# A chunk-selecting attention kernel with a routed expert layer: key transposes moved, one score unit split over column tiles, chunk sums at full height

## The chip, the cores and the metric

The kernel runs on one core of one Trainium2 chip. The metric is the device time of one execution in microseconds (us). The compute engines of the core run beside each other and wait for one another through semaphores: TensorE (PE; its weight loads are PEld), VectorE (DVE), ScalarE (ACT), GpSimd (POOL). SyncE (SP) issues transfers.

## The reference, cut to what matters

Attention first, for 4 batches of 8 heads with 768 positions of 64 numbers. Keys are cut into 24 chunks of 32. For each query an upper bound of its score with each chunk is made from the chunk's least and greatest key; the 6 best causal chunks are kept, and the softmax runs over these alone. Then every token (512 numbers, 3072 tokens) goes to the one of 8 experts that its gate prefers.

```python
k_chunks = k.reshape(B, H, nc, chunk, D)
k_min, k_max = np.min(k_chunks, axis=3), np.max(k_chunks, axis=3)
ub = np.sum(np.maximum(q[..., None, :] * k_min[:, :, None], q[..., None, :] * k_max[:, :, None]), axis=-1)
top_chunks = np.argsort(np.where(causal, ub, -1e9), axis=-1)[..., -6:]
scores = np.where(sel & causal_positions, scale * q @ k.T, -1e9)
attn_out = softmax(scores) @ v
# ...
expert_idx = np.argmax(x @ w_gate, axis=1)
out[tokens of e] = gate * (np.maximum(x @ w1[e], 0) @ w2[e])
```

Since max(q a, q b) = (q (a + b) + |q| |a - b|) / 2, the bound is made (twice as large, which changes no order) by two matmuls: q with the chunk sums max + min, and |q| with the chunk differences max - min.

## The kernel before: the parts that the change touches

The attention goes over 16 pairs of heads. The main loop runs through pair i in four groups g of work, and prepares the next pairs in between: `prep` steps of pair i+1 (bounds `ub`, `select`, `mask`) and of pair i+2 (transposes of k and q, and `kse`, the chunk sums), and router steps of earlier pairs. The order of the instructions of TensorE, GpSimd and SyncE is that of the program text. VectorE and ScalarE are put in order by the scheduler of the kernel's framework, which goes by the order in the text and by when it reckons that the inputs are there; only at the start and in the last pair do they, too, follow the text.

The tiles with tag "m" are PSUM tiles of a pool with three buffers, those with tag "s" (scores) have two, and "o" (output) one. The steps of `prep`, indented less, and the score units:

```python
    def k_half(hf):
        if hf == 0:
            s["kmx"] = work.tile([128, NCH], FP32, tag="kmx", name="kmx")
            s["kmn"] = work.tile([128, NCH], FP32, tag="kmn", name="kmn")
        pt = ps_m.tile([128, 384], FP32, tag="m")
        for t in range(3):
            nc.tensor.transpose(pt[:, ts(t, 128)], s["k"][:, 3 * hf + t], ident_f[:])
        pk = pt[:].rearrange("p (c w) -> p c w", w=CH)
        nc.vector.tensor_reduce(s["kmx"][:, ts(hf, 12)], pk, AX.X, ALU.max)
        nc.vector.tensor_reduce(s["kmn"][:, ts(hf, 12)], pk, AX.X, ALU.min)
        nc.scalar.activation(kte[0:64, 0, ts(hf, 384)], pt[0:64, :], AF.Copy, bias=0.0, scale=0.125)
        nc.scalar.activation(kte[0:64, 1, ts(hf, 384)], pt[64:128, :], AF.Copy, bias=0.0, scale=0.125)

    def kse():
        for hd in range(2):
            r = slice(64 * hd, 64 * hd + 64)
            c = slice(32 * hd, 32 * hd + NCH)
            nc.vector.tensor_tensor(ks[r, c], s["kmx"][r, :], s["kmn"][r, :], ALU.add)
            nc.vector.tensor_tensor(kd[r, c], s["kmx"][r, :], s["kmn"][r, :], ALU.subtract)

    def ub():
        pu = ps_m.tile([128, 384], FP32, tag="m")
        for w_, nm in ((ks, "qT"), (kd, "qA")):
            x_ = s[nm][:].rearrange("p a c -> p (a c)")
            for h in range(2):
                nc.tensor.matmul(pu[64 * h:64 * h + 64, 0:320], lhsT=w_[:], rhs=x_[:, ds(128 + 320 * h, 320)],
                                 start=(nm == "qT"), stop=(nm == "qA"), skip_group_check=True)
        s["ubT"] = work.tile([128, 384], FP32, tag="ud", name="ubT")
        nc.scalar.activation(s["ubT"][:, 0:320], pu[:, 0:320], AF.Copy)


    def select():
        pt = ps_m.tile([128, 3, 2, 2, 32], FP32, tag="m")
        for t in range(3):
            nc.tensor.transpose(pt[:, t], s["ubT"][:, ds(c0s[t], 128)], ident_f[:])
        ubm = work.tile([128, 3, 2, 2, NCH], FP32, tag="ubm")
        nc.vector.tensor_tensor(ubm[:].rearrange("p n h d c -> p (n h) d c"),
                                pt[:].rearrange("p n h d c -> p (n h) d c")[:, :, :, 0:NCH],
                                cbias[:].rearrange("p n h c -> p (n h) c").unsqueeze(2)
                                .to_broadcast([128, 6, 2, NCH]), ALU.add)
        top8 = work.tile([128, 3, 2, 2, 8], FP32, tag="top8")
        for t in range(3):
            for hf in range(2):
                for hd in range(2):
                    nc.vector.max(out=top8[:, t, hf, hd], in_=ubm[:, t, hf, hd])
        u3 = ubm[:].rearrange("p a b c n -> p (a b c) n")
        t3 = top8[:].rearrange("p a b c n -> p (a b c) n")
        nc.vector.tensor_tensor(nsel[:].rearrange("p a b c n -> p (a b c) n")[:, :, 0:NCH], u3,
                                t3[:, :, TOPK - 1:TOPK].to_broadcast([128, 12, NCH]), ALU.is_lt)

    def mask():
        pt = ps_m.tile([64, S], BF16, tag="m")
        for hf in range(2):
            for t in range(3):
                nc.tensor.transpose(pt[:, ds(128 + 320 * hf + c0s[t], 128)],
                                    nsel[:, t, hf].rearrange("p a n -> p (a n)"), ident_b[:])
        nc.scalar.activation(qsb[64:64 + NCH, 0, 128:S], pt[0:NCH, 128:S], AF.Copy)
        nc.scalar.activation(qsb[64:64 + NCH, 1, 128:S], pt[32:32 + NCH, 128:S], AF.Copy)

    units = [(0, [(0, 384, 0)]), (0, [(1, 256, 0), (2, 128, 256)]),
             (1, [(0, 384, 0)]), (1, [(1, 384, 0)]), (1, [(2, 384, 0)]), (1, [(3, 384, 0)]),
             (1, [(4, 256, 0), (5, 128, 256)])]

    def scores(i, u):
        kte, qsb = KTE[i % 2], QSB[i % 2]
        qb, parts = units[u]
        ps = ps_s.tile([128, 2, 512], FP32, tag="s", name="ps")
        if u in (0, 2):
            P = work.tile([128, 2, 384], FP32, tag="Pa", bufs=4, name="Pa")
        else:
            P = work.tile([128, 2, 384], FP32, tag="Pr", bufs=4, name="Pr")
        st[i][f"P{u}"] = P
        pvs = []
        for n, (kb, w, c0) in enumerate(parts):
            if len(parts) == 1:
                pv = ps[:, :, 0:w]
            else:
                pv = ps[:, n, 0:2 * w].rearrange("p (a w) -> p a w", a=2)
            for hd in range(2):
                nc.tensor.matmul(pv[:, hd, :], lhsT=kte[:, hd, ts(kb, 128)],
                                 rhs=qsb[:, hd, ds(qb * 384 + 384 - w, w)],
                                 start=True, stop=True, skip_group_check=True)
            pvs.append(pv)
        for pv, (kb, w, c0) in zip(pvs, parts):
            nc.scalar.activation(P[:, :, ds(c0, w)], pv, AF.Exp)
        for n, (kb, w, c0) in enumerate(parts):
            if kb >= 3 * qb:
                pd = P[:, :, ds(c0, 128)]
                nc.gpsimd.affine_select(out=pd, in_=pd, pattern=[[0, 2], [1, 128]],
                                        compare_op=ALU.is_ge, fill=0.0, base=0, channel_multiplier=-1)

    def attend(i, u):
        s = st[i]
        qb, parts = units[u]
        P, vt = s[f"P{u}"], s["v"]
        first, last = u in (0, 2), u in (1, 6)
        if first:
            s["po"] = ps_o.tile([128, 384], FP32, tag="o", name="po")
        po = s["po"]
        for n, (kb, w, c0) in enumerate(parts):
            for hd in range(2):
                nc.tensor.matmul(po[64 * hd:64 * hd + 64, 384 - w:384], lhsT=vt[:, kb, hd, :],
                                 rhs=P[:, hd, ds(c0, w)], start=first,
                                 stop=last and n == len(parts) - 1, skip_group_check=True)
        if last:
            ot = work.tile([128, 384], FP32, tag="ot", bufs=3)
            nc.vector.tensor_copy(out=ot[:], in_=po[:])
            s[f"ot{qb}"] = ot
        if first:
            s[f"acc{qb}"] = P
        else:
            acc = s[f"acc{qb}"]
            for n, (kb, w, c0) in enumerate(parts):
                nc.vector.tensor_tensor(acc[:, :, 384 - w:384], acc[:, :, 384 - w:384],
                                        P[:, :, ds(c0, w)], ALU.add)
```

The ranking of the tokens of a batch, of which the loop runs one in the second pair of each batch after the first (pairs 5, 9 and 13):

```python
    def rank():
        oh = bst[b]["oh"]
        of = oh[:].rearrange("p u e -> p (u e)")
        pr = ps_m.tile([128, 128], FP32, tag="m")
        nc.tensor.matmul(pr[:, 0:48], lhsT=U128[:], rhs=of, start=True, stop=False,
                         skip_group_check=True)
        for u in range(1, 6):
            nc.tensor.matmul(pr[:, 8 * u:48], lhsT=ones_b[:], rhs=of[:, 0:48 - 8 * u],
                             start=False, stop=(u == 5), skip_group_check=True)
        for u in range(6):
            nc.tensor.matmul(pr[:, 64:64 + E], lhsT=ones_b[:], rhs=oh[:, u, :],
                             start=(u == 0), stop=(u == 5), skip_group_check=True)
        rk = work.tile([128, 6, E], FP32, tag="sh")
        nc.vector.tensor_tensor(rk[:], pr[:, 0:48].rearrange("p (u e) -> p u e", e=E),
                                base_e[:].unsqueeze(1).to_broadcast([128, 6, E]), ALU.add)
        nc.vector.tensor_tensor(rk[:], rk[:], oh[:], ALU.mult)
        sl = work.tile([128, 6], FP32, tag="sl")
        nc.vector.tensor_reduce(sl[:], rk[:], AX.X, ALU.add)
        sli = work.tile([128, 6], I32, tag="sli", bufs=2)
        nc.vector.tensor_copy(out=sli[:], in_=sl[:])
        nc.vector.tensor_tensor(base_e[:], base_e[:], pr[:, 64:64 + E], ALU.add)
        bst[b]["sli"] = sli
```

The loop, for one pair (cut after the scatters), where `groups` is (0, 1), (2, 3), (4, 5), (6,):

```python
    for g in range(4):
        if g == 0:
            scores(i, 2)
            scores(i, 3)
            run(rout, i - 2, "x1")
        elif g == 1:
            scores(i, 4)
            scores(i, 5)
            if hp == 1 and b > 0:
                route[b - 1][1]()
            run(prep, i + 1, "select")
        elif g == 2:
            scores(i, 6)
            if i == NP - 1:
                for j in range(XB, 2 * XB):
                    meta(j - XB)
                    gather(j)
                    if j < len(x_slots):
                        x_in(j)
            run(prep, i + 2, "k0")
            run(prep, i + 1, "mask")
        else:
            run(rout, i - 1, "lgp", "x0")
            if i + 1 < NP:
                scores(i + 1, 0)
                scores(i + 1, 1)
            run(prep, i + 2, "k1", "q0", "q0e", "q1")
            if i + 3 < NP:
                load(i + 3, "k", "q")
        for u in groups[g]:
            attend(i, u)
        if g == 3:
            run(prep, i + 2, "q1e", "kse")
        if g == 0:
            run(prep, i + 1, "ub")
            flush()
            if 0 < i < NP - 1:
                load(i + 1, "v")
        if g == 3 and hp == 0 and b > 0:
            flush(sums_)
            route[b - 1][0]()
        if g == 1:
            run(rout, i - 1, "ud")
        if 1 <= hp <= 2 and b > 0 and spread[4 * (hp - 1) + g]:
            route[b - 1][2](spread[4 * (hp - 1) + g])
# ...
```

## Time and profile before

| | |
|---|---|
| time, median of 3 runs | 360.15 us (359.7 to 360.66) |
| span of the profiled execution | 358.6 us |
| attention, pairs 0 to 15 | up to about 250 us |
| expert layer, TensorE busy in 19 to 20 of each 20 us | 260 to 340 us |
| mean granted TensorE clock | 0.992 of full speed |

The profile's page gives first the busy time of every engine, then groups of instructions by line. "L298" is line 298 of the kernel, the score matmul in `scores`; L303 is its exp, L307 the causal select, L320 the value matmul, L325 the eviction of its result, L332 the adding up of the weights; L205 to L210 are `k_half`, L215 to L227 the same for q, L233 and L234 `kse`, L241 and L244 `ub`, L249 to L262 `select`, L269 to L272 `mask`, L348 to L356 the router's sums `ud`, L361 to L388 `lgp` and `xr`, L432 to L448 `rank`, with `oh` made in L411. A timeline row has the start, the length, the engine, the line, what is written from what, and how many instructions are merged in it; in brackets stands the idle time ahead of it and what ended that. A matmul's shape is given as rows by columns of its weights, and then that of the moving operand. A busy TensorE is not TensorE at its peak, because the ends of pipelined matmuls are modelled; the starts are measured.

### The profile page before, as it was taken

Reading aid. Unit: us, or ns where it says so; the run is one execution under the profiler, and the core shown is the slowest. Engines: PE = TensorE matmul, PEld = TensorE weight load, DVE = VectorE, ACT = ScalarE, POOL = GpSimd, SP = SyncE. Lnnn points to the kernel's source line nnn. Section 1 sums busy time; section 2 is a strip of 40 time slices with the busy share of each in tenths; the row PEclk is TensorE's granted clock in tenths of the full one; section 3 lists DMA queues with packets and bytes.
Section 4 is the critical chain, followed back from the end, with each engine's and each line's share of the span. In section 5 each row is a group of like instructions: output and inputs, shape, how many; then the busy total and the mean of one; then the engine's idle time right before and its main releaser. Section 6 shows DMA issues by size and latency. Waiting matters only on the chain. (4 is left out here: it accounts for less than half of the span.)

```text
span 358.6 us, 7585 instructions
## 1 busy us (share of the span) xinstructions
PE 326.9 (91%) x2312; PEld 171.5 (48%) x2312; DVE 235.0 (66%) x815; ACT 231.2 (64%) x398; POOL 180.4 (50%) x296
## 2 busy tenths in 40 slices
PE   6679999999899999999999988998799999999990
PEld 5535455455455465554554545443344344444430
DVE  5799889889999898999988999846460000000000
ACT  2497797797687897867977967642344444445440
POOL 3075425445474453466534547575577665653331
PEclk9999999999999999999999999999999999999996
DMA  8619998999957999937989973476999999998851
GB/s 153 112 26 194 210 220 139 215 167 215 207 127 151 182 176 195 202 100 178 200 134 212 187 148 113 73 135 116 165 211 233 221 237 197 203 186 201 157 126 48
DMA packets 138215, 59.83 MB, mean 167 GB/s; under 512 B 122811, under 2 KB 131005, under 8 KB 138176
## 3 DMA queue, kind: packets, MB, share of 16 engines
q1 hardware_dynamic: 119072, 29.52, 45.4%
q0 software_dynamic: 17536, 29.42, 42.0%
q10 hardware_dynamic: 1568, 0.39, 0.6%
q8 instruction: 21, 0.34, 0.4%
q14 instruction: 18, 0.15, 0.2%
HBM read 56.14 MB, written 10.51 MB: 186 GB/s over the span
## 5 line engine op out<-in xcount | busy, mean ns | idle before, releaser
L332 DVE TENSOR_TENSOR Pa<-Pa,Pr 128x768 f32<-128x768 f32 (+2 forms) x112 | 81.6, 729 | 1.1
L307 POOL TENSOR_SCALAR_AFFINE_SELECT Pr<-Pr 128x256 f32<-128x256 f32 x80 | 33.5, 437 | 67.3 <-ACT Pr L303 66.1
L303 ACT ACTIVATE Pr<-ps 128x768 f32<-128x768 f32 (+2 forms) x112 | 65.0, 630 | 3.2 <-PE ps L298 2.9
L612 PE MATMUL py<-w_all,hT 128*128 x224 | 52.7, 379 | 2.7 <-DMA hT<-h__3653 1.9
L298 PE MATMUL ps<-QSB,KTE 128*128 128x384 bf16 (+2 forms) x288 | 50.4, 292 | 1.2 <-DVE QSB L711 0.2
L620 POOL DMA_INDIRECT out_dram<-y,ti_all x28 | 27.8, 993 | 30.2 <-ACT y L619 26.3
L298 PEld LDWEIGHTS <-KTE 128*128 128x128 bf16 x288 | 24.1, 97 | 27.3 <-issue 21.2
L612 PEld LDWEIGHTS <-hT 128*128 128x128 bf16 x224 | 21.8, 98 | 29.5 <-DMA hT<-h__3653 2.3
L619 ACT ACTIVATE y<-py,gt_all 128x512 f32<-128x512 f32 x27 | 18.6, 687 | 20.8 <-PE py L612 18.4
L454 POOL DMA_INDIRECT xs_dram<-xrow,sli x24 | 26.9, 1121 | 7.7 <-issue 5.0
L356 ACT ACTIVATE ud<-pu 128x384 f32<-128x384 f32 x16 | 7.9, 492 | 32.8 <-PE pu L353 30.7
L303 ACT ACTIVATE Pa<-ps 128x768 f32<-128x768 f32 x32 | 26.0, 812 | 3.8 <-PE ps L298 3.2
L601 PE MATMUL ph<-w_all,KTE 128*128 x120 | 28.4, 379 | 0.0
L169 POOL DMA_DIRECT2D w_all<-in_moe_w_dram x32 | 24.3, 760 | 0.0
L307 POOL TENSOR_SCALAR_AFFINE_SELECT Pa<-Pa 128x256 f32<-128x256 f32 x16 | 6.4, 398 | 35.3 <-ACT Pa L303 35.3
L601 PE MATMUL ph<-w_all,QSB 128*128 x96 | 22.7, 379 | 0.3 <-issue 0.3
L575 DVE TENSOR_TENSOR ti_all<-xgqA,inv_i 128x1 int32<-128x1 int32 x9 | 1.4, 159 | 29.6 <-DMA xgqA<-xs_dram,grow 29.6
L554 POOL DMA_INDIRECT xgqA<-xs_dram,grow x14 | 14.6, 1046 | 10.2 <-issue 3.3
L554 POOL DMA_INDIRECT xgqT<-xs_dram,grow x14 | 14.5, 1033 | 8.7 <-DVE gt_all L577 4.9
L325 DVE COPY ot<-po 128x384 f32<-128x384 f32 x32 | 17.7, 553 | 1.6 <-PE po L320 0.9
L575 DVE TENSOR_TENSOR ti_all<-xgqT,inv_i 128x1 int32<-128x1 int32 x8 | 1.3, 159 | 26.5 <-DMA xgqT<-xs_dram,grow 26.5
L226 POOL CAST QSB<-qT 64x384 bf16<-64x384 f32 x30 | 16.3, 551 | 4.1 <-DVE qT L224 2.8
(311 smaller groups left out, 665.0 us busy)
## 6 DMA issues: line engine op xcount, KB each, us to landing
w_all<-in_moe_w_dram POOLq DMA_DIRECT2D x32, 512.0 KB, 6.0
out_dram<-y,ti_all POOLq DMA_INDIRECT x28, 3.6
t__122<-in_k_dram SPq DMA_DIRECT2D x2, 192.0 KB, 3.5
t__125<-in_q_dram ACTq DMA_DIRECT2D x2, 192.0 KB, 4.0
t__128<-in_v_dram SPq DMA_DIRECT2D x2, 192.0 KB
t__196<-in_k_dram SPq DMA_DIRECT2D x2, 192.0 KB, 3.1
t__206<-in_q_dram SPq DMA_DIRECT2D x2, 192.0 KB, 3.8
t__209<-in_v_dram SPq DMA_DIRECT2D x2, 192.0 KB
```

Source lines behind the costliest of these rows:

```text
L169: nc.gpsimd.dma_start(out=dst, in_=src.rearrange("(c p) f -> p c f", p=128))
L298: nc.tensor.matmul(pv[:, hd, :], lhsT=kte[:, hd, ts(kb, 128)], rhs=qsb[:, hd, ds(qb * 384 + 384 - w, w)], start=True, stop=True, skip_grou ...
L303: nc.scalar.activation(P[:, :, ds(c0, w)], pv, AF.Exp)
L307: nc.gpsimd.affine_select(out=pd, in_=pd, pattern=[[0, 2], [1, 128]], compare_op=ALU.is_ge, fill=0.0, base=0, channel_multiplier=-1)
L325: nc.vector.tensor_copy(out=ot[:], in_=po[:])
L332: nc.vector.tensor_tensor(acc[:, :, 384 - w:384], acc[:, :, 384 - w:384], P[:, :, ds(c0, w)], ALU.add)
L454: d = nc.gpsimd.indirect_dma_start(out=xs_dram[:], out_offset=bass.IndirectOffsetOnAxis(ap=sli[:, u:u + 1], axis=0), in_=bst[b][f"xrow{u % ...
L554: d = nc.gpsimd.indirect_dma_start(out=xg_bufs[j % XB].bitcast(I32), out_offset=None, in_=xs_dram[:], in_offset=bass.IndirectOffsetOnAxis( ...
L601: nc.tensor.matmul(ph[:, fh, :], lhsT=xT[:, c, :], rhs=w_all[:, ds(wo + (c * F + fh * 512), 512)], start=(c == 0), stop=(c == NDC - 1), sk ...
L612: nc.tensor.matmul(py[:], lhsT=hT[:, c, :], rhs=w_all[:, ds(wo + (W1W + c * DM), DM)], start=(c == 0), stop=(c == NFC - 1))
L619: nc.scalar.activation(y[:], py[:], AF.Copy, bias=0.0, scale=fs[j]["gt"])
L620: d = nc.gpsimd.indirect_dma_start(out=out[:], out_offset=bass.IndirectOffsetOnAxis(ap=fs[j]["ti"], axis=0), in_=y[:], in_offset=None, bou ...
```

## The change

It has three parts, and a rewriting that makes them possible: every step that had matmuls and evictions in one function is cut into a matmul part (`_mm`), a VectorE part (`_v`) and a ScalarE part (`_a`), so that their order can be set one by one.

- **Key transposes.** The transposes of the first half of the keys of pair i+2 go from group 2, between the scores of unit 6 and the masks, to group 1, behind the transposes of the selection. In a ranking pair the rank matmuls now follow both; they stood ahead of the selection. The VectorE work is in the text in the order selection, rank, key reductions.
- **The last score unit.** Unit 6 is computed in halves of 64 keys, each a matmul of 64 weight columns into 64 partitions of PSUM: eight matmuls for four. [...] In units 1 and 6 the two parts of the scores now lie side by side for each head, so that one exp over 128x768 takes the place of two.
- **Chunk sums.** Two full-height operations make max + min and max - min of both heads, and a third multiplies both by a 0/1 mask of the heads `bm` into one tile of block form. There were four of half height.

The exponentials of the router's gate (`ex`) take a buffer with another tag, and its steps after the one-hot are a function of their own, `gates`, that comes after all of it.

The diff, cut to its core; `s`, `ts` and `ds` are as above, and what is left out only renames or cuts functions:

```diff
+        def kse():
+            kt2 = work.tile([128, 2, NCH], FP32, tag="top8", name="kt2")
+            nc.vector.tensor_tensor(kt2[:, 0], s["kmx"][:], s["kmn"][:], ALU.add)
+            nc.vector.tensor_tensor(kt2[:, 1], s["kmx"][:], s["kmn"][:], ALU.subtract)
+            nc.vector.tensor_tensor(ksd[:, :, :, 0:NCH], kt2[:].unsqueeze(2).to_broadcast([128, 2, 2, NCH]),
+                                    bm[:].unsqueeze(1).to_broadcast([128, 2, 2, NCH]), ALU.mult)
+
 # ...
-        def kse():
-            for hd in range(2):
-                r = slice(64 * hd, 64 * hd + 64)
-                c = slice(32 * hd, 32 * hd + NCH)
-                nc.vector.tensor_tensor(ks[r, c], s["kmx"][r, :], s["kmn"][r, :], ALU.add)
-                nc.vector.tensor_tensor(kd[r, c], s["kmx"][r, :], s["kmn"][r, :], ALU.subtract)
-
 # ...
-    def scores(i, u):
+    def scores(i, u, split=False):
         kte, qsb = KTE[i % 2], QSB[i % 2]
         qb, parts = units[u]
         ps = ps_s.tile([128, 2, 512], FP32, tag="s", name="ps")
+        n = 64 if split else 128
+        for kb, w, c0 in parts:
+            for hd in range(2):
+                for h in range(128 // n):
+                    nc.tensor.matmul(ps[ds(h * n, n), hd, ds(c0, w)], lhsT=kte[:, hd, ds(kb * 128 + h * n, n)],
+                                     rhs=qsb[:, hd, ds(qb * 384 + 384 - w, w)],
+                                     start=True, stop=True, skip_group_check=True)
 # ...
-        for pv, (kb, w, c0) in zip(pvs, parts):
-            nc.scalar.activation(P[:, :, ds(c0, w)], pv, AF.Exp)
-        for n, (kb, w, c0) in enumerate(parts):
+        nc.scalar.activation(P[:], ps[:, :, 0:384], AF.Exp)
+        for kb, w, c0 in parts:
 # ... in the loop, groups 1 and 2; groups 0 and 3 keep the order of their matmuls:
                 elif g == 1:
                     scores(i, 4)
                     scores(i, 5)
-                    if hp == 1 and b > 0:
-                        route[b - 1][1]()
-                    run(prep, i + 1, "select")
+                    run(prep, n, "sel_mm")
+                    run(prep, m, "k_mm", 0)
+                    if router:
+                        rank_mm()
+                    run(prep, n, "sel_v")
+                    if router:
+                        rank_v()
+                    run(prep, m, "k_v", 0)
+                    run(prep, m, "k_a", 0)
+                    av(i, 2)
+                    av(i, 3)
+                    add(i, 3)
+                    run(rout, i - 1, "ud")
                 elif g == 2:
-                    scores(i, 6)
+                    scores(i, 6, True)
 # ...
-                    run(prep, i + 2, "k0")
-                    run(prep, i + 1, "mask")
+                    run(prep, n, "mask")
+                    av(i, 4)
+                    av(i, 5)
+                    add(i, 4)
+                    add(i, 5)
 # ... and at the end of group 3 (av, o_ev and add are attend, cut in three):
-                for u in groups[g]:
-                    attend(i, u)
-                if g == 3:
-                    run(prep, i + 2, "q1e", "kse")
 # ...
+                    av(i, 6)
+                    o_ev(i, 1)
+                    add(i, 6)
+                    run(prep, m, "kse")
+                    if hp == 0 and b > 0:
+                        flush(sums_)
+                        route[b - 1][0]()
+                        route[b - 1][1]()
 # ...
```

## The prediction, made before the changed kernel was run

> **What bounds the kernel now.** I read the shares of busy time first, then the busy time by stretch cut at the head pairs, then the timelines of TensorE, VectorE and ScalarE inside one ordinary pair and one pair that also ranks tokens for the router.
>
> ```profile
> PE 326.9 (91%) x2312; PEld 171.5 (48%) x2312; DVE 235.0 (66%) x815; ACT 231.2 (64%) x398; POOL 180.4 (50%) x296
> ```
>
> Over the whole span TensorE leads, but the last 100 us are the expert matmuls, which the change does not touch. The attention part has to be looked at by pairs. A pair is marked by its first chunk-bound matmul (line 241); the windows below go from mark to mark, and their columns are length, then busy time of PE, PEld, DVE, ACT and POOL.
>
> ```profile
> 77.60:91.30 13.70, 13.62 (x114) 7.48 (x112) 12.66 (x40) 11.40 (x22) 6.37 (x14) 1.00 1.14 200
> 91.30:107.20 15.90, 14.44 (x123) 7.65 (x119) 15.21 (x56) 11.66 (x23) 9.17 (x15) 1.00 0.73 153
> ...
> 205.00:222.40 17.40, 14.39 (x126) 7.93 (x122) 16.57 (x69) 12.97 (x25) 10.35 (x16) 1.00 0.59 127
> ```
>
> An ordinary pair lasts 13.7 us and TensorE is busy in 13.6 of it: it is the bound there, and VectorE has 1.0 us to spare, ScalarE 2.3. A pair that ranks the batch before it (there are three: pairs 5, 9 and 13) lasts 16.0 us, or 17.4 with the table steps in it; there VectorE is busy 15.2 of 15.9 and TensorE has gaps. So I reckon the two kinds of pair separately: about 11 ordinary ones count, and the three others hold 2.3 + 2.3 + 3.7 = 8.3 us over 13.7 each.
>
> The timeline of TensorE in the ranking pair shows the gaps (start, length, line, what ended the idle time):
>
> ```profile
> 92.42 1.06 PE L298 MATMUL ps<-QSB,KTE 128*128 128x384 bf16 x4
> 94.02 0.20 PE L432 MATMUL pr<-oh,U 128*128 128x48 bf16 x1 [0.54 <-DVE oh L411]
> ...
> 97.68 0.50 PE L205 MATMUL pt<-ident_f,t__1357 128*128 128x128 f32 x3
> 98.97 0.47 PE L269 MATMUL pt<-ident_b,nsel 128*64 128x128 bf16 x5 [0.79 <-DVE nsel L262]
> ```
>
> TensorE waits twice for VectorE: for the one-hot `oh` ahead of the rank matmuls, and for the selection `nsel` ahead of the mask transposes. In the raw starts the first costs 0.86 us where a score matmul is otherwise followed in 0.16, so 0.70; the second 1.06 instead of 0.20, so 0.86. Together 1.56 us a pair. An ordinary pair has neither wait.
>
> [...] Three key transposes followed by more of full width take 116.43 - 116.08 = 0.35 us; the same three ahead of 64-column mask transposes take 0.43:
>
> ```profile
> 112.12 0.50 PE L298 MATMUL ps<-QSB,KTE 128*128 128x256 bf16 x4
> 112.46 0.50 PE L205 MATMUL pt<-ident_f,t__1606 128*128 128x128 f32 x3
> 112.89 0.47 PE L269 MATMUL pt<-ident_b,nsel 128*64 128x128 bf16 x5
> ...
> 116.08 0.52 PE L205 MATMUL pt<-ident_f,t__1606 128*128 128x128 f32 x3
> 116.43 0.95 PE L215 MATMUL pt<-ident_f,t__1609 128*128 128x128 f32 x6
> ```
>
> [...] the mean bf16 weight load is 97 ns for 128 columns (line 298) and 109 ns for only 64 (line 269), so a column costs about twice as much. [...] the KS sum at 63.17 takes 0.48 us beside a GpSimd cast from 63.11 to 63.61, where the one at 62.90 takes 0.16.
>
> **Part 1, transposes moved and score unit split.** In group 2 TensorE now goes from 32-column router sums to full-width scores (unit 6) and key transposes and then to 64-column masks: [...] Cost of group 2 from the scores' start to the masks: now 112.89 - 112.12 = 0.77 us. After: four pairs of halves. Two halves of 64 columns in different column tiles run side by side (the two heads of the value matmuls start 7 ns apart in the raw starts), so the streams take what they take now, 0.34 us, unless the weight loads hold them: the masks stream one 64-column weight every 56 ns, so two need 112 ns, and the two narrow pairs (56 ns of stream each) may wait. Estimate 0.38 us, at worst 4 x 0.11 = 0.45. The key transposes go to group 1, behind the selection's, and cost 0.35 there. Saved 0.77 - 0.38 - 0.35 = 0.04 us a pair; over 15 pairs 0.6 us, and it could be 0.5 us the other way. I count zero.
>
> **Part 2, what follows in the ranking pairs.** The selection's transposes now stand ahead of the rank matmuls, and the key transposes between them. The selection therefore no longer waits for `oh`, and the rank matmuls come about 0.45 + 0.35 = 0.8 us later, when `oh` is there (it was 0.70 late). On VectorE the selection is traced ahead of the rank sums; now these stand before it (94.51 to 95.12), and an accumulation of 0.96 us stands inside it. The gate operations come after the one-hot instead of between its steps. Both waits should go, 1.56 us a pair; I leave 0.2 for VectorE, which is full there and only loses its kse time. Three pairs: -4.1 us. In pair 13 the transposes of q wait 1.5 us more for the router's VectorE work; -0.5 us for that.
>
> **Part 3, chunk sums.** Now four half-height operations:
>
> ```profile
> L233 DVE TENSOR_TENSOR KS<-kmx,kmn 64x24 f32<-64x24 f32 x32 | 11.3, 354 | 0.3
> ...
> L234 DVE TENSOR_TENSOR KD<-kmx,kmn 64x24 f32<-64x24 f32 x32 | 7.6, 237 | 0.0
> ```
>
> That is 18.9 us in 16 pairs, 1.2 us a pair. Undisturbed, one takes 0.16 us and the next starts after 0.09. Three full-height ones, of 24, 24 and 96 elements, are two of 0.09 and one like the 128x96 product of line 367 (two of those in 0.41), so 0.2: some 0.4 us, or 0.7 beside a GpSimd cast. VectorE gains 0.5 to 0.8 us a pair. In ordinary pairs that is off the path: the bound matmuls do not wait for KS or KD (they follow the value matmuls in 0.10 us). At the start of the kernel the first bound matmul does wait for them: -0.5 us. In the ranking pairs it is part of what part 2 needs.
>
> The single exp of units 1 and 6 takes 0.81 instead of a pair of 0.87; ScalarE gains 0.12 us a pair, which nothing waits for. The bm constants are GpSimd fills at the start, in front of nothing.
>
> **Part 4, the new pressure.** The key half's evictions on ScalarE (lines 209 and 210) now stand behind the mask copies; afterwards they are traced, and ready, ahead of them.
>
> ```profile
> 112.31 0.49 ACT L356 ACTIVATE ud<-pu 128x384 f32<-128x384 f32 x1 [1.77 <-PE pu L353]
> 112.70 0.87 ACT L303 ACTIVATE Pr<-ps 128x512 f32<-128x512 f32 x2
> 113.59 0.69 ACT L271 ACTIVATE QSB<-pt 24x640 bf16<-24x640 bf16 x1
> 114.29 0.69 ACT L272 ACTIVATE QSB<-pt 24x640 bf16<-24x640 bf16 x1
> 115.01 0.48 ACT L209 ACTIVATE KTE<-pt 64x384 bf16<-64x384 f32 x1
> ```
>
> The next pair's scores start at 115.42 and their second head at about 115.59; the second mask copy ends at 114.99, 0.6 us early. Moving two evictions of 0.5 us ahead makes it end at about 116.0, 0.4 us late, if they start only when router sums and exp are ready too. They can start after the key reductions, at about 112.5 in this pair (selection from 109.67, 2.0 us of its own, and two reductions of 0.47). The 1.77 us idle stretch before 112.31 is missed by a little. So an ordinary pair may become 0 to 0.5 us longer; I take 0.25, and 11 x 0.25 = +2.75 us.
>
> **Sum.** -4.1 - 0.5 - 0.5 + 2.75 = -2.35 us; 360.15 gives 357.8, say **358 us**.
>
> **The rivals.** *ScalarE takes the place*: the mask copies wait behind the key evictions in every pair. For it speaks the margin of 0.6 us against 1.0 us of moved work; against it the 1.77 us gap. At its full 0.5 us: 11 x 0.25 more, about 361. *VectorE stays the bound of the ranking pairs*: 15.2 us of work less 0.8 is still 14.4, so at most 1.5 of the 2.3 us can be had; if adds are still put inside the selection, half of it: about 360. *TensorE gains in all pairs*: if the split halves load free and nothing new waits, ordinary pairs become 0.1 us shorter and the ranking pairs go to 14.1: about 353. *The split costs*: weight loads not overlapped, 0.4 us a pair: about 364.
>
> **Range and chances.** These give 353 to 364; I put the range at 353 to 365. Two per cent is 7.2 us. Faster by that needs nearly all of the 8.3 us of excess, 0.10; slower needs 0.5 us or more in every pair and no gain in the ranking ones, 0.10; within 2% 0.80.
>
> **What would show it.** In the profile after: the pitch of ordinary pairs 13.7 to 14.1; TensorE's wait for `oh` and `nsel` gone from pairs 5, 9 and 13, which come to 14.3 to 14.8 us; the three kse operations at some 0.4 us a pair; the second mask copy ending after the next pair's first scores if rival one is right, with TensorE waiting for it. I am wrong if the order of VectorE and ScalarE comes out otherwise than traced, or if the score halves do not run side by side.

## The result and the profile after

The changed kernel takes **372.27 us** (371.79 to 374.37, 4 runs) against 359.92 us of the kernel before (358.9 to 360.66, 4 runs): a ratio of 1.0356, 95% interval 1.0308 to 1.0405. It is slower by 12.4 us, where 358.0 was predicted and 365 was the end of the range.

The page of the kernel after, shares of busy time, the granted TensorE clock in 40 slices of the span, and the groups of VectorE's adding up, GpSimd's causal select and ScalarE's eviction of the keys. Line numbers have moved: L337 was L332, L316 was L307, L216 was L209 and L210, L303 was L298, L285 was L271 and L272, L205 is still the key transposes, L232 those of q, L249 the bound matmuls.

```profile
PE 331.6 (90%) x2366; PEld 175.7 (47%) x2376; DVE 237.2 (64%) x799; ACT 229.6 (62%) x366; POOL 186.9 (51%) x297
...
PEclk9996999999999999999999999899999999999996
...
L337 DVE TENSOR_TENSOR Pa<-Pa,Pr 128x768 f32<-128x768 f32 (+2 forms) x112 | 86.8, 776 | 5.1 <-PE po L329 1.3
L316 POOL TENSOR_SCALAR_AFFINE_SELECT Pr<-Pr 128x256 f32<-128x256 f32 x80 | 39.5, 514 | 92.0 <-ACT Pr L312 92.0
...
L216 ACT ACTIVATE KTE<-pk 64x384 bf16<-64x384 f32 x60 | 29.1, 485 | 31.5 <-DVE kmn L211 29.1
```

No engine's busy time explains 12 us: TensorE has 4.7 us more, GpSimd 6.5 more (the select above had 33.5), VectorE 2.2 more (the adds had 81.6), ScalarE 1.6 less. So the waits have to be read. The digit 6 in the fourth slice of the clock is new and comes up again below.

The busy time by stretch, columns as in the prediction (length, then busy time of PE, PEld, DVE, ACT, POOL; then clock, DMA share, GB/s): an ordinary pair, the ranking pair 5, and two stretches at a lower clock, inside pair 0 and pair 13.

```profile
84.34:98.43 14.09, 13.76 (x113) 7.64 (x115) 12.62 (x39) 11.16 (x19) 6.92 (x13) 1.00 1.13 194
98.43:114.31 15.88, 14.32 (x128) 7.89 (x125) 15.35 (x53) 12.22 (x23) 9.02 (x14) 1.00 0.84 179
...
28.67:35.50 6.83, 6.24 (x31) 3.67 (x33) 4.28 (x6) 2.77 (x5) 0.96 (x3) 0.50 0.63 106
...
230.06:233.47 3.41, 3.41 (x16) 1.87 (x15) 2.31 (x9) 2.53 (x5) 3.17 (x5) 0.50 0.26 74
```

From mark to mark, up to the last mark, that of pair 14 (the last column adds up, but for rounding, to the 12.5 us by which this mark comes later; behind it 1.0 is made good):

| | before, us | after, us | difference in all |
|---|---|---|---|
| start to pair 0 | 23.2 | 23.1 | -0.1 |
| pair 0 | 13.25 | 18.03 | +4.8 |
| ten ordinary pairs, mean | 13.66 | 14.29 | +6.3 |
| ranking pairs 5 and 9, each | 15.96 | 15.88 | -0.2 |
| pair 13, with the table steps | 17.39 | 19.03 | +1.6 |

The waits of TensorE in the kernel after (engine, tile and line, what it waited for, total us, times, longest):

```profile
PE ps L303 <- ACT QSB L285: 4.1, 13, 0.4
PE pq L232 <- ACT KTE L216: 3.8, 2, 2.2
PE pk L205 <- DMA t__385<-in_k_dram: 3.6, 1, 3.6
PE pu L249 <- DVE KSD L223: 2.6, 3, 1.5
```

The two waits of the kernel before, for `oh` and for `nsel`, are not in this list. In their place: the scores wait in nearly every pair for the masks, the key transposes once for a load, and q's transposes and the bound matmuls for ScalarE and VectorE.

**An ordinary pair.** The timeline of TensorE (start, length; pair 6, its mark at 114.31) around the end of unit 6 and the first scores of the next pair:

```profile
119.55 0.52 PE L303 MATMUL ps<-QSB,KTE 128*64 128x256 bf16 x8
119.91 0.44 PE L282 MATMUL pm<-ident_b,nsel 128*64 128x128 bf16 x5
...
122.34 0.33 PE L303 MATMUL ps<-QSB,KTE 128*128 128x384 bf16 x1
122.97 0.65 PE L303 MATMUL ps<-QSB,KTE 128*128 128x384 bf16 x5 [0.30 <-ACT QSB L285]
```

The first head's score matmul goes; the second head waits for its mask. ScalarE's timeline says why:

```profile
119.28 0.98 ACT L216 ACTIVATE KTE<-pk 64x384 bf16<-64x384 f32 x2 [1.63 <-DVE kmn L211]
...
121.51 1.41 ACT L285 ACTIVATE QSB<-pm 24x640 bf16<-24x640 bf16 x2
```

The two evictions of the first key half now stand at the head of the row, and the second mask copy ends at 122.92, 8.61 us after the pair's mark; in the ordinary pair that the prediction shows (mark at 107.20) it ended at 114.99, 7.78 after. The idle stretch ahead of the row did not take in the evictions. ScalarE waits through it, for the least-key reduction (L211) of the same tile: on the page, 29.1 of the 31.5 us of idle time ahead of this line. The two evictions themselves take 0.98 us, 0.49 each.

VectorE in the kernel before, in the pair that the prediction shows, and in this pair of the kernel after:

```profile
112.42 0.95 DVE L332 TENSOR_TENSOR Pa<-Pa,Pr 128x768 f32<-128x768 f32 x1
113.29 0.55 DVE L207 TENSOR_REDUCE kmx<-pt 128x12 f32<-128x384 f32 x1
```

```profile
117.16 0.55 DVE L210 TENSOR_REDUCE kmx<-pk 128x12 f32<-128x384 f32 x1
...
118.65 0.54 DVE L211 TENSOR_REDUCE kmn<-pk 128x12 f32<-128x384 f32 x1
...
119.47 3.30 DVE L337 TENSOR_TENSOR Pa<-Pa,Pr 128x768 f32<-128x768 f32 x3
```

The key reductions have moved into the selection, and the three large adds, which stood one here and one there between other steps, now follow one another on one tile. In the raw starts each starts 1.06 us after the one before; where another step followed it, the kernel before needed 0.87 (112.42 to 113.29), and the third add here, beside a GpSimd select, takes 1.19. The router's product `lgt`, which q's transposes wait for (it frees their PSUM buffer), starts 9.20 us after the mark instead of 8.71, and q's transposes at 9.71 instead of 9.23. So there are two waits in an ordinary pair, one of about 0.45 us made by ScalarE (the scores' second head starts 0.63 us after the first, where 0.17 is usual) and one of 0.23 made by VectorE. A third, of 0.22, stands at the end of six of the ten ordinary pairs: the bound matmuls start 0.33 us after the last value matmul, where it was 0.10. The chunk sums, VectorE again, are what comes last there (the times are under `e1_k_back` below). A reordering that the list of the change's parts leaves out may bear on this: VectorE's and ScalarE's parts of q's second half (`q1e` in the kernel before) now stand ahead of the value matmuls of unit 6, as `f4_best` below undoes.

**Pair 0.** From the timeline of SyncE's issues (SPq is its row of transfers; the three issues that begin at 23.37, 24.15 and 24.86 us here follow one another):

```profile
24.86 1.13 SPq L191 DMA_DIRECT2D t__385<-in_k_dram  x2
```

The keys of pair 2 are issued at 24.9 us, behind two transfers of gate weights, the first of which waits 13.0 us for a constant of GpSimd by SyncE's own list of waits (`SPq L148 <- POOL tokid L154: 13.0, 1, 13.0`). Pair 0 wants those keys in group 2 in the kernel before, in group 1 after: the transposes start at 29.26, after 3.6 us of waiting. From 28.67 to 35.50 the granted clock is 0.50 (the third line of the windows above), so that the pair loses 4.8 us and not 3.6. The trace of the kernel before has the warning in its list of TensorE's waits. The keys were issued at 24.72 there, and even in group 2 the transposes waited for them, until 28.61; there was no slack at all to move them forward:

```profile
PE pt L205 <- DMA t__386<-in_k_dram: 0.5, 1, 0.5
```

Pair 13 shows the same on a smaller scale: q's transposes wait 2.2 us for ScalarE's key eviction (the longest wait of the second line above), which itself comes after a key reduction of VectorE, and from 230.06 to 233.47 the clock is 0.50 (the fourth line of the windows). In the kernel before they waited 1.2 us there, for `lgt` (`PE pt L215 <- DVE lgt L367: 1.2, 1, 1.2`), and the pair's clock was 1.00.

### The profile page after: what moved, and what is told of

Same layout as the page of the kernel before. It is cut to its first block, busy times and chain, and to the rows that moved or that the text cites. A ratio compares the mean times of both kernels' runs of the same rounds, so it can differ in the third digit from the quotient of the medians.

```text
span 370.1 us, 7616 instructions
## 1 busy us (share of the span) xinstructions
PE 331.6 (90%) x2366; PEld 175.7 (47%) x2376; DVE 237.2 (64%) x799; ACT 229.6 (62%) x366; POOL 186.9 (51%) x297
## 5 line engine op out<-in xcount | busy, mean ns | idle before, releaser
L337 DVE TENSOR_TENSOR Pa<-Pa,Pr 128x768 f32<-128x768 f32 (+2 forms) x112 | 86.8, 776 | 5.1 <-PE po L329 1.3
L316 POOL TENSOR_SCALAR_AFFINE_SELECT Pr<-Pr 128x256 f32<-128x256 f32 x80 | 39.5, 514 | 92.0 <-ACT Pr L312 92.0
L312 ACT ACTIVATE Pr<-ps 128x768 f32<-128x768 f32 x80 | 63.4, 811 | 2.6 <-PE ps L303 2.6
L303 PE MATMUL ps<-QSB,KTE 128*128 128x384 bf16 (+4 forms) x352 | 52.0, 290 | 5.0 <-ACT QSB L285 4.1
L216 ACT ACTIVATE KTE<-pk 64x384 bf16<-64x384 f32 x60 | 29.1, 485 | 31.5 <-DVE kmn L211 29.1
L644 POOL DMA_INDIRECT out_dram<-y,ti_all x28 | 27.8, 993 | 30.2 <-ACT y L643 24.9
L303 PEld LDWEIGHTS <-KTE 128*128 128x128 bf16 (+1 forms) x352 | 25.3, 103 | 32.6 <-issue 27.1
L210 DVE TENSOR_REDUCE kmx<-pk 128x12 f32<-128x384 f32 x32 | 17.6, 549 | 7.9 <-PE pk L205 7.8
L285 ACT ACTIVATE QSB<-pm 24x640 bf16<-24x640 bf16 x30 | 20.8, 692 | 0.8
L272 DVE MAX8 top<-ubm 128x8 f32<-128x24 f32 x192 | 18.5, 168 | 0.1
```

Of the source, the lines that this page charges most:

```text
L216: nc.scalar.activation(kte[0:64, hd, ts(hf, 384)], pt[64 * hd:64 * hd + 64, :], AF.Copy, bias=0.0, scale=0.125)
L285: nc.scalar.activation(qsb[64:64 + NCH, hd, 128:S], pt[32 * hd:32 * hd + NCH, 128:S], AF.Copy)
L303: nc.tensor.matmul(ps[ds(h * n, n), hd, ds(c0, w)], lhsT=kte[:, hd, ds(kb * 128 + h * n, n)], rhs=qsb[:, hd, ds(qb * 384 + 384 - w, w)], s ...
L312: nc.scalar.activation(P[:], ps[:, :, 0:384], AF.Exp)
L644: d = nc.gpsimd.indirect_dma_start(out=out[:], out_offset=bass.IndirectOffsetOnAxis(ap=fs[j]["ti"], axis=0), in_=y[:], in_offset=None, bou ...
```

## The experiments

### The move of the key transposes undone

`e1_k_back`: the kernel after, with the first key half's steps where they had been.

```diff
-                    run(prep, m, "k_mm", 0)        # group 1, behind sel_mm
-                    run(prep, m, "k_v", 0)
-                    run(prep, m, "k_a", 0)
+                    # the same three in group 2, ahead of "mask"
```

> The changed kernel with the key transposes of the first half, their reductions and their evictions put back into group 2, ahead of the masks; the split of unit 6, the new chunk sums and the new place of the rank matmuls stay. Theory 1 (ScalarE: the key evictions stand ahead of the mask copies, so the next pair's scores wait 0.42 to 0.46 us in every pair, and the router's transposes and the bounds follow late) and theory 2 (the keys are needed one group earlier and their transfer has not landed: 3.8 us in pair 1 and 2.2 us in all later) both put all of the loss into this move: 357 to 361 us. Theory 3 (the split score unit loads its weights badly) leaves it at 370 or more. Theory 4 (the three full-height sums collide with GpSimd) leaves it at 368 or more.

360.57 us (12 runs) against 361.05: 0.9996 (0.9956 to 1.0035). **With the move undone the whole loss is gone**; what is left of the change comes out even. Pair 0 is back at 13.04 us, and the ranking pairs 5 and 9 at 14.76 where they were 15.96, just where the prediction put them. This is not a gain because ordinary pairs have a mean of 13.94 against 13.66. ScalarE's row has the old order again, the masks ahead of the keys:

```profile
72.22 1.40 ACT L285 ACTIVATE QSB<-pm 24x640 bf16<-24x640 bf16 x2
73.64 0.98 ACT L216 ACTIVATE KTE<-pk 64x384 bf16<-64x384 f32 x2
```

but in six of the ten the bound matmuls start 0.47 us after the last value matmul, where it was 0.10. The lists of waits name two things, an eviction of q for the weight load (`PEld pu L249 <- ACT QSB L242: 3.0, 8, 0.4`) and the chunk sums for the matmul (`PE pu L249 <- DVE KSD L223: 1.2, 6, 0.2`).

The raw ends decide for the sums: the weight load starts 0.115 us after the last of them in pair 3 of this kernel, and just so in that of the kernel after, of `h1_no_kev`, `f4_best` and `g1_pin`, whereas q's last finished eviction lies anywhere from 0.03 to 0.9 us back.

Per part, by the marks: ten ordinary pairs +2.8 us, ranking pairs -1.2 - 1.2 - 0.6, pair 0 -0.2, the stretch up to pair 0 +1.4. Against this kernel, the move costs 3.6 us in ordinary pairs, 5.0 in pair 0 and 4.5 in the three ranking pairs: 13.1. The stretch up to pair 0 is 1.5 us longer here than in the kernel after, but the edit does not touch it: its length goes from 23.0 to 25.0 us over the traces, and `f1_before_k0` (24.8) and `f2_before_rank` (23.2) have the same text there.

### The move alone, in the kernel before

`f1_before_k0`: before, with the step `k0` (transposes, reductions and evictions together) from group 2 to group 1.

```diff
                     run(prep, i + 1, "select")
+                    run(prep, i + 2, "k0")
                 elif g == 2:
...
-                    run(prep, i + 2, "k0")
                     run(prep, i + 1, "mask")
```

> The kernel before with one thing changed: the step k0 (transposes, reductions and evictions of the first key half) stands in group 1 behind the selection. Theories 1 (key evictions ahead of the mask copies on ScalarE, and the PSUM buffer that they hold) and 2 (keys not landed): the move alone makes the kernel slower by 8 to 12 us: 368 to 372 us, with the scores' wait for the mask copies and the wait for the keys of pair 2 in its trace. If the loss needs the other parts too (adds thrown together beside GpSimd, the sums): 363 us or less.

368.56 us against 360.66: 1.0217 (1.0156 to 1.0278). The move alone costs 7.9 us (5.6 to 10.0 by the interval). Its waits of TensorE are the two of the kernel after:

```profile
PE ps L298 <- ACT QSB L272: 3.8, 13, 0.4
PE pt L205 <- DMA t__386<-in_k_dram: 2.8, 1, 2.8
```

Ordinary pairs have 14.11 us, pair 0 17.18. In the ranking pairs 5 and 9 it gains 0.6 each and in pair 13 0.9, where the whole change has nearly nothing or loses. So by the marks the move costs 6.3 us in the pairs of the old kernel (3.9 + 4.5 - 2.1), and 13.1 in the pairs of the new one: about half of the loss comes only together with the other edits, nearly all of that in the ranking pairs.

### The evictions behind the masks

`e2_ka_late`: after, with only ScalarE's part `k_a(0)` written behind `mask`. The scheduler still put one of the two evictions ahead.

```diff
                     run(prep, m, "k_v", 0)
-                    run(prep, m, "k_a", 0)
...
                     run(prep, n, "mask")
+                    run(prep, m, "k_a", 0)
```

> The changed kernel with the transposes and reductions left in group 1, but the two key evictions on ScalarE written behind the mask copies; the built order has one of the two still ahead, in ScalarE's idle stretch, and one behind. Theory 1: the wait of the scores' second head goes from 0.45 to under 0.1 us, and about 5 to 9 us come back: 363 to 367 us, the rest being the landing of the keys. Theory 2 alone: no gain, 371 to 373 us.

370.92 us against 361.05: 1.0271 (1.0197 to 1.0346). The 5 to 9 us that were expected back did not come; ordinary pairs have a mean of 14.30 us, as in the kernel after. The scores' wait is gone and another is there, 0.3 us per pair: transposes of the router take the PSUM buffer that the masks hold, and wait for the mask copy.

```profile
PE px L400 <- ACT QSB L285: 3.4, 11, 0.6
```

The second mask copy of pair 6 still ends 8.09 us after the mark, for 7.78 before the change; the wait moved on from the reader of the masks to the next user of their buffer.

### Without the evictions

`h1_no_kev`: after, with pair 2's keys loaded early as in `f3_load2` below, and **with the evictions of the first key half left out** from pair 2 on. Its scores use old keys; the time is that of the same kernel with 0.98 us less work on ScalarE per pair.

```diff
-        consts_last()
         load(2, "k", "q")
+        consts_last()
...
-                    run(prep, m, "k_a", 0)
```

> The changed kernel with the early loads of pair 2, and with the two evictions of the first key half on ScalarE left out from pair 2 on (those keys stay what they were two pairs earlier, so the output is not the reference's); VectorE's order is that of the changed kernel. Theory 1 (ScalarE's 1.0 us ahead of the mask copies): the scores no longer wait, ordinary pairs go from 14.1 to 14.5 down to 13.6 to 13.8, the total to 360 to 363 us. Rival (VectorE's order: three adds together beside GpSimd's selects, the router's product late): ordinary pairs stay above 14.0 and the total above 365 us.

365.0 us (20 runs) against 361.03: 1.0102 (1.0072 to 1.0133); `f3_load2`, which differs by the evictions alone, has 1.0201. So they account for some 3.6 us, by two intervals that just touch. Ordinary pairs come to 14.02 us from 14.33, not to 13.66. The scores' wait is gone, and the wait of q's transposes, whose records name the transposes ahead of it although VectorE's `lgt` is what ends just before, has grown from 0.23 to 0.47 us in the raw starts:

```profile
PE pq L232 <- PE pk L205: 4.6, 11, 1.0
```

With ScalarE's part taken away, VectorE's is the limit, and half of the gain is lost to it.

### The load of pair 2's keys earlier, and the move undone in one pair

`f3_load2`: after, `load(2, "k", "q")` issued ahead of `consts_last()`, which holds the gate weights (the first hunk of the diff above).

> The changed kernel with the loads of k and q of pair 2 issued ahead of the two small transfers of the gate weights, which wait for GpSimd's constants until 23 us. Theory 2: the 3.8 us wait of TensorE for these keys, which lies in pair 0, goes, and with it about 4.5 us: 367 to 368 us. Theory 1 alone: 371 to 373 us.

368.23 us against 360.66: 1.0201 (1.0132 to 1.027), where the kernel after has 1.0356. Pair 0 takes 13.71 us instead of 18.03 and its granted clock is 1.00, in this one line of the windows:

```profile
23.70:37.40 13.70, 11.03 (x86) 6.16 (x84) 12.56 (x43) 10.53 (x18) 9.60 (x25) 1.00 0.59 93
```

That is 4.3 us, of a loss of 12.4, and pair 13 has 0.6 less too. Ordinary pairs stay at 14.33.

`e5_pair1_back` was meant to show the same, with the move undone for one pair.

```diff
-                    run(prep, m, "k_mm", 0)
+                    if i != 1:
+                        run(prep, m, "k_mm", 0)
...                                        # k_v, k_a likewise; for i == 1 in group 2
```

> The changed kernel, with the key transposes put back into group 2 in pair 1 alone, where they waited 3.8 us for the keys to land. Theory 2: pair 1 goes from 18.0 us to about 13.5, the total to 367 to 368 us, with the other pairs as they were (14.1 to 14.8). Theory 1 alone: only a small part, 371 to 373 us.

370.95 us against 361.05: 1.0313 (1.0238 to 1.0388). I had taken the wrong pair. The keys that land late are asked for in pair 0; the wait of 3.2 us stayed, and the run does not test that cause. Pair 1 itself came to 14.10 us from 14.48, as in `e1_k_back` (14.11).

### Selection ahead of the rank matmuls, alone

`f2_before_rank`: before, with the selection traced ahead of the rank step.

```diff
+                    run(prep, i + 1, "select")
                     if hp == 1 and b > 0:
                         route[b - 1][1]()
-                    run(prep, i + 1, "select")
```

> The kernel before with the selection ahead of the rank step in group 1, nothing else. If the wait for the one-hot and the wait for the selection were the excess of the three ranking pairs, they go from 16.0 to 14.8 us: 356 to 358 us. If VectorE is what bounds those pairs: within 1 us of before.

360.61 us (20 runs) against 360.66: 0.9989 (0.9965 to 1.0014). Both waits, for `oh` and `nsel`, are gone, 1.56 us by the prediction's count. Pairs 5 and 9 went from 15.96 to 15.60, and pair 13 from 17.39 to 17.76, with 3.4 us of it at a granted clock of 0.50 (0.90 in its mean). The rest came back later in the same pair, as a wait of the transposes of q:

```profile
102.31 0.96 PE L215 MATMUL pt<-ident_f,t__1360 128*128 128x128 f32 x6 [0.88 <-PE pt L205]
```

They start 1.04 us late by the raw starts, and `lgt` is again what ends just before. VectorE bounds these pairs, and the order of TensorE's waits does not matter much. The further 0.84 us which `e1_k_back` has there come with less busy time of VectorE, 14.05 us in pair 5 against 15.03 here (sums and rewriting; no run parts the two).

### The split undone

`e3_no_split`: after, unit 6 in four full-width matmuls.

```diff
-                    scores(i, 6, True)
+                    scores(i, 6)
```

> The changed kernel with unit 6 in four full-width matmuls, all else left. Theory 3: back to 362 or less. Theories 1 and 2: the split is worth about 0.1 us a pair either way: 371 to 375 us[...].

372.85 us against 361.05: 1.036 (1.0262 to 1.0459), within this interval the same as with it; ordinary pairs have 14.34 us for 14.29. In the kernel after, the halves take 119.91 - 119.55 = 0.36 us where four full matmuls took 0.34; 0.38 was the prediction's estimate.

### Towards a better kernel

`f4_best`: the three repairs together: keys back, pair 2's load early, and VectorE's and ScalarE's parts of q's second half behind the value matmuls of unit 6, as before.

```diff
                     # keys back in group 2 and load(2) early, as above, and
-                    for hf in range(2): q_mm(hf), q_v(hf), q_a(hf)
+                    q_mm(0), q_v(0), q_a(0), q_mm(1)
...
                     add(i, 6)
+                    run(prep, m, "q_v", 1)
+                    run(prep, m, "q_a", 1)
                     run(prep, m, "kse")
```

> The changed kernel with the key step back in group 2, the second evictions of q behind the value matmuls of unit 6 as before the change, and the early loads of pair 2. The 0.4 us wait of the bound matmuls for a PSUM buffer that the evictions of q hold goes from two of three ordinary pairs, the wait for keys in pair 0 too, and the ranking pairs stay at 14.8: 354 to 357 us. If ordinary pairs stay at 14.0: 359 to 361 us.

365.11 us against 360.66: 1.0128 (1.0069 to 1.0186). A miss. Ordinary pairs are at 13.8 us as hoped, but for one, pair 6, at 15.24, and the ranking pairs 5 and 9 are at 16.6 to 16.8, longer than before. TensorE's and VectorE's timelines of one of them:

```profile
111.23 0.76 PE L249 MATMUL pu<-qT,KSD 128*64 128x320 f32 x4 [2.14 <-DVE KSD L223]
```

```profile
110.36 0.56 DVE L405 TENSOR_TENSOR xrow<-px,rec 128x384 bf16<-128x384 f32 x1 [1.59 <-issue]
110.84 0.25 DVE L223 TENSOR_TENSOR KSD<-kt,bm 128x96 f32<-128x96 f32 x1
```

The scheduler put the router's product `xrow` between the second and the third chunk sum. It waits 1.59 us, and the bound matmuls behind it, whose wait of 2.1 us has a lower clock after it in pair 6 (a mean of 0.62 from 111.20 to 114.90). The profile names nothing that it waits for; a scatter of earlier rows that still reads `xrow` fits, but that is argued and not shown.

`g1_pin` is the kernel after with keys back and q's second half late, and the second `xrow` product held to the order of the text; `g3_q1late_oldsums` has keys back and q late, with four half-height sums in place of the product by `bm`.

```diff
+            if hf == 1 and i < NP - 3:             # g1_pin
+                tc.keep_in_program_order(d)        # d: the xrow product
```

```diff
-            nc.vector.tensor_tensor(kt2[:, 0], s["kmx"][:], s["kmn"][:], ALU.add)
-            # ... subtract, and the product by bm
+            for hd in range(2):                    # g3_q1late_oldsums
+                r = slice(64 * hd, 64 * hd + 64)
+                nc.vector.tensor_tensor(ksd[r, 0, hd, 0:NCH], s["kmx"][r, :], s["kmn"][r, :], ALU.add)
+                nc.vector.tensor_tensor(ksd[r, 1, hd, 0:NCH], s["kmx"][r, :], s["kmn"][r, :], ALU.subtract)
```

> The changed kernel with the key step back in group 2, the second evictions of q behind the value matmuls of unit 6, and the product into xrow pinned behind the chunk sums on VectorE, so that it cannot stand between them and wait for a scatter that still reads its buffer. If that was the 2.1 us wait of the bound matmuls in the ranking pairs, these go from 16.6 to 14.8 us and ordinary pairs stay at 13.8: 356 to 359 us, faster than both. If the wait moves on: 361 to 365 us.

> The changed kernel with the key step back in group 2, the late second evictions of q, and four half-height chunk sums in place of three full-height ones. If the third, dependent operation is what lets another instruction in between, the ranking pairs come to 15.0 to 15.6 us and ordinary ones to 13.7: 357 to 360 us. If the sums make no difference: as with the three operations in this order, 364 to 366 us.

`g1_pin`: 367.62 us against 361.03, 1.0151 (1.0074 to 1.0229), above both ranges that were expected. `g3_q1late_oldsums`: 364.19 against 361.03, 1.0049 (1.0003 to 1.0096). Holding `xrow` back took the long wait away, the ranking pairs 5 and 9 have 15.9 us, but the sums themselves were late: the bound matmuls wait for `KSD` in nine pairs, 5.0 us in all, and two ordinary pairs in three have 14.29 us or a little more. With the old sums, most ordinary pairs are even, 13.82 us, and ranking pairs have 15.3, as expected; but the total is not. The profiled execution was the fastest, 360.75 us, so the profile does not show where the 3.4 us lie by which the median is above it. No kernel of mine is faster than the kernel before.

## Why the prediction was wrong, point by point

- **The step that failed first is part 1, "I count zero".** It weighed the times of the matmuls and did not ask when the keys are there. In pair 0 they were not: 4.8 us in the kernel after, 4.3 of it given back by an earlier load alone (`f3_load2`). The kernel before had waited 0.5 us for the same keys one group later, so the slack was nil and could be read beforehand. The keys of later pairs land just in time or 0.1 to 0.8 us late.
- **Part 4 had the right mechanism and the wrong size.** The evictions came ahead of the mask copies and made the second head wait, as rival one had it. The term was "I take 0.25, and 11 x 0.25 = +2.75 us". Its own working had given 0.4 (a copy that ends at 116.0 for scores due at 115.59) and was then nearly halved; in the raw starts the scores of most ordinary pairs waited 0.42 to 0.47 us. The 1.77 us gap that spoke against it was not to be had, since ScalarE spends it waiting for the reductions. And the ordinary pairs lost 0.63, because VectorE's order changed too: its two waits, for `lgt` and for the chunk sums, were in no step. `f1_before_k0`, with the move alone, has ScalarE's wait and neither of these; `h1_no_kev`, without the evictions, has not ScalarE's, but a longer wait for `lgt`. The raw starts of pair 7 part the three (us from one matmul's start to the next, at the scores' second head, at q's first transpose and at the first bound matmul):

  | run | scores | q | bounds | pair 7 |
  |---|---|---|---|---|
  | before | 0.17 | 0.11 | 0.10 | 13.66 |
  | after | 0.58 | 0.34 | 0.33 | 14.22 |
  | move alone, `f1_before_k0` | 0.54 | 0.11 | 0.10 | 14.00 |
  | no evictions, `h1_no_kev` | 0.17 | 0.55 | 0.15 | 14.05 |
  | move undone, `e1_k_back` | 0.17 | 0.20 | 0.48 | 14.00 |
  | old sums, q late too, `g3_q1late_oldsums` | 0.17 | 0.20 | 0.10 | 13.82 |

- **Part 2, -4.1 us, came to -0.2 in pairs 5 and 9 together, and pair 13 lost 1.6.** The waits for `oh` and `nsel` went, as predicted, which by itself is worth only 0.4 us a pair (`f2_before_rank`), as rival two said: VectorE stays the bound. In the kernel after, other waits filled what was left: in pair 5 the scores 0.4, the bound matmuls 0.8 for the chunk sums; in pair 13 q's transposes 2.2 instead of 1.2, with the lower clock after it, where the prediction had put -0.5 us down. Without the move the pairs came to 14.76, within "14.3 to 14.8". The step was right for a change that it was not part of.
- **Part 3 was mis-sized as well, and its path did not hold**: three operations "some 0.4 us, or 0.7 beside a GpSimd cast". In the lines by form (busy us in all, mean ns):

```profile
L221 DVE TENSOR_TENSOR kt<-kmx,kmn 128x24 f32<-128x24 f32 x16 | 8.1, 508 | 0.0
L223 DVE TENSOR_TENSOR KSD<-kt,bm 128x96 f32<-128x96 f32 x16 | 5.1, 316 | 0.2
```

  With the 2.7 us of the subtraction that makes 15.9 us, 1.0 a pair, against 18.9 before: 0.2 saved for 0.5 to 0.8 predicted. The first one takes most of the blows (0.17 us alone, up to 1.25). The -0.5 us at the start of the kernel came to -0.1. And "off the path" in ordinary pairs did not hold after the change: in six of ten the bound matmuls now wait for the last sum, as the table above has it.
- **Right**: the split (0.36 for 0.38 us, and no effect in `e3_no_split` that its interval of 1% either way would show), and the two waits that went.
- **The range** was wrong because all its ends came from one pair at a time. I had multiplied a wait by eleven, and never looked at the one pair in which the steps run without their stock of loaded data.

## What to carry to other kernels

When matmuls are moved forward, move with them in thought everything that hangs on their PSUM tile: the load that feeds them (in the first iterations above all), the reductions, and the evictions, which then stand ahead of other work in their engine's row (here the second mask copy ended 8.61 us after the mark instead of 7.78). Reckon each engine's row anew by time after a fixed mark; an idle stretch there can be used only if what is moved is ready in it (the evictions waited through 1.63 us of it for a reduction). A removed wait on an engine that was not the bound of its stage brought little here (0.4 us a pair of 1.56 in `f2_before_rank`), and a wait taken away moved on to the next user of the same buffer (0.3 us a pair in `e2_ka_late`): try the one-line move alone before the whole change.

## What the runs showed of the hardware

- **TensorE's clock after a wait.** In the kernel after the granted clock is 1.00 or 0.50, and up to 340 us it changes at 28.67, 35.50, 230.06 and 233.47 us, whole multiples of 3.41 us apart. What follows goes by steps of this length up to 340 us (idle time as the profile has it; ends of matmuls are modelled). In the kernel after TensorE idled for 3.0 us in the step ahead of the first slow stretch (25.26 to 28.67, in pair 0), and for 2.25 in that ahead of the second (226.65 to 230.06, in pair 13). Every other step at full clock, in this kernel and in the one before, had 1.54 us of idle time or less, and none of these was followed by a slow one. The slow step from 28.67 on, with 0.59 us of idle time, was followed by a second; the other two slow ones, with none, by full clock. Other runs show the same: after a wait of 2.84 us in `f1_before_k0` the clock was 0.50 from 30.90 to 34.60, and 2.14 us in `f4_best` were followed by the mean of 0.62 given there. So a step need not be idle throughout; 2.25 of its 3.41 us were enough here. Pair 0 takes 18.03 us in the kernel after, with two slow steps after a wait of 3.6; 16.70 in `e5_pair1_back`, with a mean clock of 0.66 from 29.30 to 33.00 after one of 3.2; and the pair 0 without such a wait (`f3_load2`) ran at 1.00. As an estimate from these figures, a slow step costs at most half of 3.41 us, 1.7; in pair 0 of the kernel after 4.8 us were lost for 3.6 of waiting, 1.2 more.
- **A small operation caught by a long one.** In pair 5 the first chunk sum, 0.17 us alone, takes from 112.32 to 113.57:

```profile
112.32 1.25 DVE L221 TENSOR_TENSOR kt<-kmx,kmn 128x24 f32<-128x24 f32 x1
```

  GpSimd adds two halves of the router's sums from 112.11 to 112.64 and then casts q (`QSB<-qT`) until 113.53, and the chunk sum ends with them. It is of full height and stays 1.25 us all the same; in all, three operations took 15.9 us where four had taken 18.9. What the sums take in pair 5 goes with the length of this pair, in us: 1.87 and 15.96 before, 1.66 and 15.89 after, 1.51 and 15.60 in `f2_before_rank`, 0.98 and 15.37 in `f1_before_k0`, 0.78 and 14.76 in `e1_k_back`. No run changes the meeting with GpSimd alone, so that it sets the length of these pairs is not shown.
- **Narrow weights side by side.** Eight score matmuls of 64 weight columns went through in 0.36 us, four of 128 in 0.34 (112.12 to 112.46 in the kernel before). In the raw starts the two halves of each of the four begin 2 to 3 ns apart, and the loads of their weights take 0.11 us each; all that the eight cost over the four is 0.02 us.
